# Rows of the first transform stored in thirds of the frequencies, native fp32 for half of the first batch's units, and loads in another order

## The chip, the core and the metric

The kernel runs on one core of a Trainium2 chip. A core has five engines, each with its own instruction stream: TensorE (PE; loads of its stationary operand are listed as PEld), VectorE (DVE), ScalarE (ACT), GpSimd (POOL) and SyncE (SP). In the part that matters here SP issues nearly all DMAs, in program order: an instruction of SP that waits for a semaphore holds up every DMA behind it. The DMAs run on 16 shared DMA engines. The metric is the device time of one execution in microseconds (us).

## The reference, cut to what matters

The input is `x`, 8 batches of 3072 positions by 256 channels. A Fourier layer comes first, then two dense mixtures.

```python
X = np.fft.rfft(x, axis=1)
Yr = Xr @ w_r - Xi @ w_i + b_r
Yi = Xr @ w_i + Xi @ w_r + b_i
Yr, Yi = soft_threshold(Yr, 0.01), soft_threshold(Yi, 0.01)
y = np.fft.irfft(Yr + 1j * Yi, n=3072, axis=1)
# then: soft mixture of experts over all 24576 rows, then softmax(h)*h, layer norm, w_out
```

Everything is float32. The change touches the forward transform of the first batch alone.

## The kernel before

The work has two phases; the change is in the head of phase 1.

**The transform.** The 3072 positions are taken as 96 x 32, and the transform is done in two stages. `stage1` (L240) is a product with a 96 x 96 matrix: a unit is a tile of 96 partitions by 2 x 256 columns (two of the 32 values of n2), and each batch has 16 units, `pr` 0 to 15. Float32 precision is had from the faster number type fp32r: the matrix is split into `df_h` + `df_l` and x into `hi` + `lo`, and three matmuls (high-high, low-high, high-low) are summed in PSUM. `xsplit` (L222) makes `hi` and `lo`. In batch 0 an odd unit is split on DVE alone; an even unit, and every unit of later batches, has `hi` on ACT (L234) and `lo` on POOL (L235).

**Through memory.** ACT evicts the result (L261), and `a_out` (L263) stores it to a tensor `ad` in DRAM. `load_ap` (L268) reads it back with n2 on the partitions. Batch 0 stores each unit by itself (192 KB); later batches store two units together (384 KB). The 96 rows of a unit are ordered (k, g), k being 4 and g 24 frequencies. A block t (12 per batch) uses two of the 24; blocks 0 to 3 use g 0 to 7, blocks 4 to 7 use g 8 to 15, blocks 8 to 11 the rest.

**The blocks.** `stage2` (L277) is the second stage for one block: 4 native fp32 matmuls of 128 columns, each of which shows as two records on PE, into `xps`. ACT and DVE split the result. `mix` (L317) multiplies with the weights `wc_h`, `wc_l` into `pb` and `pa`, adds the biases on DVE (L339) and applies the threshold (L345 on DVE, L346 on POOL). `st_transpose` and many small steps follow, up to the mixture's softmax.

**The order.** It is written out by hand. `after(n, f)` queues step f for n ticks later, `tick()` runs what is due. The head (L784 on) does `stage1(0, pr)` for all 16 units, each time with the split of the unit three ahead, and a store of each unit at once; in between, SP's loads of weights, biases and the first constants stand at fixed units (`early`, L741), `load_x(20)` (two tiles with units 16 to 19, 384 KB each) behind unit 9, the preparation of weights on DVE (`weights`, L730) behind unit 12. Then come `load_x(22)`, `load_ap(0, 0, 0)`, a constant, `load_ap(0, 0, 1)`, and `HEAD` = 4 units of batch 1 ahead of the first block. From then on each step of the main loop does a stage2, a mix and one or two units of the next batch. x tiles of later batches have two buffers, so the load of a tile waits until POOL has subtracted both units of the tile two before.

Of the kernel before, what the change touches and what calls it, by code (L numbers as in the profile page):

```python
# [8 lines left out]
F32 = mybir.dt.float32  # L9
F32R = mybir.dt.float32r  # L10
# [25 lines left out]
def kernel(  # L36
# [25 lines left out]
    B, N, D = x.shape  # L62
# [25 lines left out]
    def mm(out, lhsT, rhs, start=True, stop=True):  # L88
        PE.matmul(out=out, lhsT=lhsT, rhs=rhs, start=start, stop=stop)  # L89
# [56 lines left out]
    def phase1(pl: ExitStack, pr_: ExitStack):  # L146
# [39 lines left out]
        def after(dq, fn, *a):  # L186
            heapq.heappush(heap, (now[0] + dq, now[1], fn, a))
            now[1] += 1
# [13 lines left out]
        ad = {}  # L202
# [20 lines left out]
        def xsplit(i):  # L223
            if i >= 16 * B:
                return
            t = xt.pop(i)
            if i < 16 and i % 2 == 1:
                hi = st_p.tile([96, 2, D], F32R, name="x0h", tag="st")
                lo = st_p.tile([96, 2, D], F32R, name="x0l", tag="st")
                split(hi, lo, t, "dve")  # L230
            else:
                z = wa_p.tile([96, 2, 2, D], F32R, name="x1", tag="x1")
                hi, lo = z[:, 0], z[:, 1]
                ACT.activation(out=hi, in_=t, func=AF.Copy)  # L234
                POOL.tensor_tensor(out=lo, in0=t, in1=hi.bitcast(F32), op=ALU.subtract)  # L235
            xs1[i] = (hi, lo)
            if i >= 16 and i % 2 == 1:
                after(LAG["load_x"], load_x, i + 5)

        def stage1(b, pr):  # L240
            ch, h = divmod(pr, 2)
            if pr == 0:
                ad[b] = dram2.tile([32, 4, 24, D], F32, name="ad", tag="ad")
            if b == 0:
                dst = s_p.tile([96, 2, D], F32, name="a0", tag="s")
                after(LAG["a_out"], a_out, b, 2 * pr, 2, dst)
            elif h == 0:
                aw[0] = wa_p.tile([96, 4, D], F32, name="asb", tag="asb")
                dst = aw[0][:, 0:2, :]
            else:  # L250
                dst = aw[0][:, 2:4, :]
                after(LAG["a_out"], a_out, b, 4 * ch, 4, aw[0])
            hi, lo = xs1.pop(16 * b + pr)
            if 16 * b + pr < 16 + HEAD and pr % 3:
                ps = (pst if pr % 3 == 1 else psm).tile([96, 2, D], F32, name="s1", tag="sps" if pr % 3 == 1 else "pm")
            else:
                ps = ps1.tile([96, 2, D], F32, name="s1", tag="s1")
            mm(ps, df_h, hi, True, False)
            mm(ps, df_l, hi, False, False)
            mm(ps, df_h, lo, False, True)  # L260
            ACT.activation(out=dst, in_=ps, func=AF.Copy)  # L261

        def a_out(b, n, k, t):  # L263
            SP.dma_start(out=ad[b][n:n + k].rearrange("n k g d -> (k g) n d"), in_=t)

        apt = {}

        def load_ap(b, q, th):  # L268
            t = ap_p.tile([128, 2, 2, D], F32, name="apt", tag="apt")
            for gp in range(2):  # L270
                g0 = 8 * q + 4 * gp + 2 * th
                SP.dma_start(out=t[:, gp], in_=ad[b].rearrange("n k g d -> (n k) g d")[:, g0:g0 + 2, :])
            apt[b, q, th] = t

        xhl = {}
# [41 lines left out]
        def mix(b, t):  # L317
# [16 lines left out]
            for s, w in ((sh, wc_h), (sh, wc_l), (sl, wc_h)):  # L334
                for dh in range(2):
                    mm(pa[:, 0, :], s[:, dh, :], w[:, dh, 512:768], n == 0, n == 5)
                    n += 1
            yb = y_p.tile([128, 2, D], F32, name="yb", tag="yb")
            DVE.tensor_tensor(out=yb, in0=pb, in1=bias0 if t == 0 else bias, op=ALU.add)  # L339

# [373 lines left out]


        dft = sm_p.tile([96, 96], F32, name="dft", tag="qt_sb", bufs=2)
        SP.dma_start(out=dft, in_=c_dft)
        load_x(16)
        POOL.memset(ones, 1.0)
        zero4 = k_p.tile([128, 2, 2, 1], F32, name="zero4")  # L720
        POOL.memset(zero4, 0.0)
        POOL.memset(r_sb[:, 24:32, :], 0.0)
        zx = sm_p.tile([128, 2, 128], F32, name="zx", tag="q_sb", bufs=2)
        POOL.memset(zx, 0.0)
        split(df_h, df_l, dft, "dve")
        SPLIT0 = LAG["split0"]
        for i in range(SPLIT0):
            xsplit(i)
# [1 line left out]
        def weights():  # L730
            wk = sm_p.tile([128, 2, 512], F32, name="wk", tag="c_sb")
            DVE.scalar_tensor_tensor(out=wk[:, :, 0:256], in0=wc[:, :, 256:512], scalar=-1.0, in1=wc[:, :, 0:256], op0=ALU.mult, op1=ALU.subtract)
            DVE.tensor_tensor(out=wk[:, :, 256:512], in0=wc[:, :, 0:256], in1=wc[:, :, 256:512], op=ALU.subtract)
            split(wc_h[:, :, 0:512], wc_l[:, :, 0:512], wk, "dve")
            split(wc_h[:, :, 512:768], wc_l[:, :, 512:768], wc[:, :, 256:512], "dve")
            for z in (xd_h, xd_l):
                DVE.tensor_copy(out=z, in_=zx)
            DVE.tensor_copy(out=bias0, in_=bias)
            DVE.tensor_copy(out=bias0[0:1, 1, :], in_=bias[0:1, 0, :])

        early = {  # L741
            3: [(wc[:, :, 0:256], w_i.rearrange("(k p) e -> p k e", p=128))],
            5: [(wc[:, :, 256:512], w_r.rearrange("(k p) e -> p k e", p=128))],
            7: [
                (bias[:, 0, :], b_r.rearrange("(o e) -> o e", o=1).to_broadcast([128, D])),
                (bias[:, 1, :], b_i.rearrange("(o e) -> o e", o=1).to_broadcast([128, D])),
            ],
            13: [(d2_sb[:, 0:2, :], c_d2[:, 0:2, :])],
        }
        late = {  # L750
            1: (ident, c_id),
            2: (d2_sb[:, 8:16, :], c_d2[:, 8:16, :]),
# [14 lines left out]
        for pr in range(16):  # L767
            stage1(0, pr)
            if pr + SPLIT0 < 16:
                xsplit(pr + SPLIT0)  # L770
            for o, i in early.get(pr, []):
                SP.dma_start(out=o, in_=i)
            if pr == 9:
                load_x(20)
            if pr == 12:
                weights()
            if pr == 14:
                xsplit(16)
            tick()
        xsplit(17)  # L780
        tick()
        s1_done = [16]
# [7 lines left out]
                if s1_done[0] == 16 * B:  # L790
                    after(2, load_wa)

        load_x(22)
        load_ap(0, 0, 0)
        load_const(d2_sb[:, 2:8, :], c_d2[:, 2:8, :])
        load_ap(0, 0, 1)
        for k in range(HEAD):
            s1_next(17 + k)
            tick()
        for k in late:  # L800
            after(k, load_const, *late[k])
        stage2(0, 0)
        stage2s(0, 0)

# [477 lines left out]
def _consts():  # L1282
# [56 lines left out]
    for cg in range(4):  # L1339
# [57 lines left out]
```

## Time and profile before

| What | us |
|---|---|
| median of 3 runs | 1346.2 (1345.92 to 1346.29) |
| the profiled execution, its own time | 1344.05 |
| its span in the trace | 1341.9 |
| PE busy | 1278.4 (95%) |
| DVE busy | 1181.0 (88%) |
| ACT busy | 1042.3 (78%) |
| POOL busy | 962.0 (72%) |
| mean granted clock of PE, share of full | 0.984 |

Times in rows are microseconds from the start of the span. Busy time of PE counts matmuls, which overlap by their pipeline; the step from one start to the next is the better measure of a matmul's rate. A row's bracket says how long the engine was idle before it and what released it. L89 is the helper through which all matmuls go, so matmuls are told apart by the tile they write: `s` is stage1, `xps` stage2, `pb` and `pa` the mix.

### The profile page before, as it was taken

The numbers are of one execution on the slowest core, as the hardware profiler recorded it, in microseconds if no ns is written. First come the engines' busy times: TensorE is split into PE (matmuls) and PEld (weight loads), VectorE is DVE, ScalarE is ACT, GpSimd is POOL, SyncE is SP. The second block draws the span as 40 slices with busy tenths as digits, with TensorE's granted clock in tenths as the row PEclk, the third lists the DMA queues.
The fourth block names the chain that finished last, engine by engine and source line by source line (L and its number), as shares of the span: only waits on it lengthen the run. The fifth ranks groups of instructions, "written<-read, shape, count | busy, mean of one in ns | idle before, by whom it ended". The sixth has DMA issues, their size and how long they took to land.

```text
span 1341.9 us, 30708 instructions
## 1 busy us (share of the span) xinstructions
PE 1278.4 (95%) x10868; PEld 1152.1 (86%) x10868; DVE 1181.0 (88%) x1670; ACT 1042.3 (78%) x2005; POOL 962.0 (72%) x1028
## 2 busy tenths in 40 slices
PE   6999999999999999888599999999999999999998
PEld 3888888888878888764398999999999999999997
DVE  7788888888898979765799999999999999999993
ACT  5567666666667665443599999999999999999995
POOL 5556574757566563231199999998999989999896
PEclk8999999999999999998799999999999999999999
DMA  8966464645546365339477787777777777777763
GB/s 264 305 202 177 120 193 122 200 131 155 162 121 185 96 197 169 96 123 350 113 173 183 193 212 197 189 195 177 202 192 202 178 186 198 190 205 178 195 170 108
DMA packets 178649, 241.69 MB, mean 180 GB/s; under 512 B 20160, under 2 KB 143296, under 8 KB 178496
## 3 DMA queue, kind: packets, MB, share of 16 engines
q1 hardware_dynamic: 178160, 238.55, 65.3%
q8 instruction: 86, 1.41, 0.5%
q10 hardware_dynamic: 336, 1.18, 0.3%
q14 instruction: 67, 0.55, 0.1%
HBM read 91.94 MB, written 59.11 MB: 113 GB/s over the span
## 4 chain that ended last, share of the span: by engine, by line
PE 72%; DVE 11%; POOL 6%; issue 5%; DMA 3%; ACT 2%; SPq 1%; POOLq 0%; DVEq 0%; ACTq 0%
PE po L89 36%; PE pb L89 7%; PE pm L89 6%; PE hps L89 6%; PE s L89 5%; PE xps L89 4%; PE pa L89 3%; POOL ul L1108 2%; POOL x L235 2%; PE sps L92 2%; DMA xc<-in_x_dram 2%; PE hps L92 1%; PE pm L92 1%; DVE xl L298 1%; DVE yb L339 1%
## 5 line engine op out<-in xcount | busy, mean ns | idle before, releaser
L1108 POOL TENSOR_TENSOR ul<-t,uh 128x512 fp32r<-128x512 f32 x338 | 433.3, 1299 | 37.2 <-ACT uh L1094 35.2
L89 PEld LDWEIGHTS po<-gw,uh 128*128 128x128 f32 x2736 | 348.7, 189 | 14.0
L89 PE MATMUL po<-gw,uh 128*128 128x256 f32 x2736 | 354.9, 281 | 0.0
L346 POOL TENSOR_TENSOR s<-yb,s 128x512 f32<-128x512 f32 x95 | 132.5, 1395 | 215.1 <-DVE s L345 183.5
L998 DVE TENSOR_REDUCE st<-hps 128x1 f32<-128x1024 f32 x192 | 229.2, 1194 | 13.3 <-PE hps L89 13.3
L89 PE MATMUL po<-gw,ul 128*128 128x256 f32 x1620 | 231.2, 285 | 7.4 <-POOL ul L1108 7.1
L1013 DVE SCALAR_TENSOR_TENSOR u<-hps,e 128x1024 f32<-128x1024 f32 x192 | 232.2, 1209 | 0.5 <-ACT e L1005 0.5
L1005 ACT ACTIVATE e<-hps,st 128x1024 f32<-128x1024 f32 x192 | 215.4, 1122 | 17.6 <-DVE st L998 17.5
L1118 ACT ACTIVATE sq<-u,st 128x1024 f32<-128x1024 f32 x192 | 222.8, 1160 | 0.2 <-DVE u L1013 0.2
L1036 DVE STREAM_TRANSPOSE tb<-u 128x1024 f32<-128x1024 f32 x169 | 210.5, 1246 | 7.3 <-DMA t<-tb 1.5
L89 PEld LDWEIGHTS po<-gw,ul 128*128 128x128 f32 x1620 | 207.0, 188 | 10.8 <-POOL ul L1108 9.4
L235 POOL TENSOR_TENSOR x<-xc,x 96x512 fp32r<-96x512 f32 x120 | 164.2, 1377 | 30.0 <-ACT x L234 28.8
L1094 ACT ACTIVATE uh<-t 128x768 fp32r<-128x768 f32 x169 | 143.4, 849 | 1.1 <-DMA t<-tb 1.1
L261 ACT ACTIVATE asb<-s 96x512 f32<-96x512 f32 x112 | 66.6, 595 | 73.0 <-PE s L89 72.9
L89 PE MATMUL hps<-gst,ct 128*128 128x512 f32 x338 | 107.5, 401 | 14.3 <-DVE u L1013 12.9
L89 PE MATMUL s<-x,df_h 96*96 96x512 f32 x240 | 104.9, 439 | 13.7 <-POOL x L235 4.8
L89 PEld LDWEIGHTS xps<-d_sb,apt 128*128 128x128 f32 x768 | 99.0, 193 | 13.2 <-issue 2.9
L89 PE MATMUL xps<-d_sb,apt 128*128 128x128 f32 x768 | 105.0, 280 | 1.5 <-DMA apt<-ad 1.4
L1095 POOL CAST uh<-t 128x256 fp32r<-128x256 f32 x169 | 68.4, 405 | 37.9 <-DMA t<-tb 37.9
L1169 ACT ACTIVATE osb<-po,st 128x256 f32<-128x256 f32 x192 | 80.3, 476 | 11.4 <-PE po L89 11.4
L234 ACT ACTIVATE x<-xc 96x512 fp32r<-96x512 f32 x120 | 75.1, 626 | 14.2 <-DMA xc<-in_x_dram 14.2
L297 DVE TENSOR_TENSOR xsum<-xps,xi 128x256 f32<-128x256 f32 x96 | 39.8, 414 | 48.1 <-ACT xh L296 44.9
(212 smaller groups left out, 2425.5 us busy)
## 6 DMA issues: line engine op xcount, KB each, us to landing
t<-tb SPq DMA_DIRECT2D x676, 128.0 KB, 2.8
apt<-ad SPq DMA_DIRECT2D x96, 256.0 KB, 4.4
out_dram<-osb SPq DMA_DIRECT2D x47, 512.0 KB, 3.8
xc<-in_x_dram SPq DMA_DIRECT2D x56, 384.0 KB, 4.1
ad<-asb SPq DMA_DIRECT2D x56, 384.0 KB, 3.5
ct<-c_dram SPq DMA_DIRECT2D x96, 128.0 KB, 4.0
wt<-in_moe_w_dram SPq DMA_DIRECT2D x21, 512.0 KB, 8.7
ws<-in_moe_w_dram SPq DMA_DIRECT2D x22, 256.0 KB, 6.0
```

What stands on the lines that cost most here:

```text
L89: PE.matmul(out=out, lhsT=lhsT, rhs=rhs, start=start, stop=stop)
L234: ACT.activation(out=hi, in_=t, func=AF.Copy)
L235: POOL.tensor_tensor(out=lo, in0=t, in1=hi.bitcast(F32), op=ALU.subtract)
L346: (DVE if last else POOL).tensor_tensor(out=s, in0=y, in1=s, op=ALU.subtract)
L998: DVE.tensor_reduce(out=st[:, 0, k:k + 1], in_=hps[i], op=ALU.min, axis=AX.X)
L1005: ACT.activation(out=e, in_=hps[i], func=AF.Exp, bias=st[:, 0, k:k + 1], scale=-1.0, accum_out=st[:, 1, k:k + 1])
L1013: DVE.scalar_tensor_tensor(out=u, in0=hps[i] if turned(i) else hps.pop(i), scalar=1.0, in1=et.pop(i), op0=ALU.mult, op1=ALU.mult, accum_ou ...
L1036: DVE.transpose(out=t, in_=ut[i])
L1094: ACT.activation(out=w[:, 0:HA], in_=v[:, 0:HA], func=AF.Copy)
L1108: POOL.tensor_tensor(out=ul[:, z, :].rearrange("p c (a j) -> p c a j", a=4), in0=v, in1=w.bitcast(F32), op=ALU.subtract)
L1118: ACT.activation(out=sq, in_=ut.pop(i), func=AF.Square, bias=st[:, 2, k:k + 1], scale=-float(DFF), accum_out=st[:, 3, k:k + 1])
L1169: ACT.activation(out=o[:, k], in_=pot.pop(i), func=AF.Copy, scale=stt[j][:, 4, k:k + 1])
```

## The change

In batch 0:

- The matrix has a second copy, `c_dft0`, with its 96 columns ordered in three thirds of 8 frequencies. The result's partitions 0 to 31 are then the first third, and so on.
- Even units are no longer split: `xsplit` hands on the loaded tile, and `stage1` does one native fp32 matmul with `dft0`. Odd units stay as they were, with the split of `dft0`.
- A unit's result is stored in three parts of 32 partitions (64 KB) to three DRAM tensors. The first third goes out at once, as the whole unit did. The second thirds of all units go out behind `load_x(22)`, ahead of the four units of batch 1; the last thirds two at a time in ticks 3 to 10 of the main loop.
- The loads of the weights and the first constant stand directly behind the x loads. `load_x(20)`, the split of `dft`, the preparation of weights and `xsplit(16)` stand behind unit 15. `load_x(22)` and the loads of the biases stand behind `load_ap(0, 0, 1)`. The two copies of biases move from `weights` into the first `mix`.

```diff
@@ xsplit
-            if i < 16 and i % 2 == 1:
+            if i < 16 and i % 2 == 0:
+                xs1[i] = (t, None)
+                return
+            if i < 16:
@@ stage1
-                after(LAG["a_out"], a_out, b, 2 * pr, 2, dst)
+                after(LAG["a_out"], a_first, 0, 2 * pr, dst)
+                firsts.append((2 * pr, dst))
...
-            mm(ps, df_h, hi, True, False)
-            mm(ps, df_l, hi, False, False)
-            mm(ps, df_h, lo, False, True)
+            wh, wl = (df_h, df_l) if b else (df0[:, 0], df0[:, 1])
+            if lo is None:
+                mm(ps, dft0, hi)
+            else:
+                mm(ps, wh, hi, True, False)
+                mm(ps, wl, hi, False, False)
+                mm(ps, wh, lo, False, True)
...
+        def a_first(q, n, t):
+            SP.dma_start(out=ad0[q][n:n + 2].rearrange("n k g d -> (k g) n d"), in_=t[32 * q:32 * q + 32])
+        ad0 = [dram.tile([32, 4, 8, D], F32, name=f"ad0_{q}") for q in range(3)]
@@ load_ap
-                SP.dma_start(out=t[:, gp], in_=ad[b].rearrange("n k g d -> (n k) g d")[:, g0:g0 + 2, :])
+                src = ad[b][:, :, 8 * q:8 * q + 8, :] if b else ad0[q]
+                SP.dma_start(out=t[:, gp], in_=src.rearrange("n k g d -> (n k) g d")[:, g0:g0 + 2, :])
@@ mix, ahead of yb
+            if (b, t) == (0, 0):
+                biases()
@@ the head
+        SP.dma_start(out=dft0, in_=c_dft0)
+        load_x(16)
         SP.dma_start(out=dft, in_=c_dft)
-        load_x(16)
+        SP.dma_start(out=wc[:, :, 0:256], in_=w_i.rearrange("(k p) e -> p k e", p=128))
+        SP.dma_start(out=wc[:, :, 256:512], in_=w_r.rearrange("(k p) e -> p k e", p=128))
+        SP.dma_start(out=d2_sb[:, 0:2, :], in_=c_d2[:, 0:2, :])
...
-            if pr == 9:
-                load_x(20)
-            if pr == 12:
-                weights()
-            if pr == 14:
-                xsplit(16)
             tick()
+        tick()
+        load_x(20)
+        split(df_h, df_l, dft, "dve")
+        weights()
+        xsplit(16)
         xsplit(17)
...
-        load_x(22)
         load_ap(0, 0, 0)
         load_const(d2_sb[:, 2:8, :], c_d2[:, 2:8, :])
         load_ap(0, 0, 1)
+        for k, z in enumerate((b_r, b_i)):
+            load_const(bias[:, k, :], z.rearrange("(o e) -> o e", o=1).to_broadcast([128, D]))
+        load_x(22)
+        for n, t in firsts:
+            a_first(1, n, t)
         for k in range(HEAD):
             s1_next(17 + k)
             tick()
...
+        for z, (n, t) in enumerate(firsts):
+            after(3 + z // 2, a_first, 2, n, t)
```

## Rows read from the trace of the kernel before

**Rows 1.** The page: busy time by engine; POOL's group of subtractions at L235.
```profile
PE 1278.4 (95%) x10868; PEld 1152.1 (86%) x10868; DVE 1181.0 (88%) x1670; ACT 1042.3 (78%) x2005; POOL 962.0 (72%) x1028
...
L235 POOL TENSOR_TENSOR x<-xc,x 96x512 fp32r<-96x512 f32 x120 | 164.2, 1377 | 30.0 <-ACT x L234 28.8
```

**Rows 2.** Busy time by stretch; columns as in the first line.
```profile
core 0: us, PE busy (x) PEld busy (x) DVE busy (x) ACT busy (x) POOL busy (x), PEclk, DMA share, GB/s
0.00:34.05 34.05, 22.08 (x61) 11.62 (x61) 24.04 (x28) 20.30 (x35) 18.75 (x21) 0.89 0.88 266
34.05:50.00 15.95, 14.66 (x104) 13.81 (x104) 10.81 (x26) 7.45 (x18) 5.63 (x5) 0.91 1.03 336
50.00:54.00 4.00, 3.62 (x27) 3.16 (x27) 3.28 (x6) 2.92 (x7) 3.64 (x4) 1.00 0.52 147
54.00:78.00 24.00, 23.17 (x182) 20.34 (x180) 20.32 (x32) 15.02 (x34) 16.60 (x13) 1.00 1.02 301
78.00:96.00 18.00, 18.00 (x153) 16.74 (x154) 15.81 (x34) 11.20 (x28) 8.17 (x7) 1.00 0.50 153
...
22.60:26.30 3.70, 0.00 (x0) 0.00 (x0) 3.60 (x6) 1.13 (x3) 0.42 (x1) 1.00 1.05 328
26.90:34.00 7.10, 5.42 (x11) 2.19 (x10) 2.46 (x4) 4.38 (x8) 5.10 (x5) 0.50 0.82 239
34.00:37.00 3.00, 2.95 (x14) 2.95 (x15) 0.00 (x0) 0.91 (x3) 1.64 (x2) 0.50 0.98 349
37.00:40.00 3.00, 1.71 (x14) 1.55 (x14) 2.55 (x11) 1.28 (x5) 0.00 (x0) 1.00 1.09 359
```

**Rows 3.** The chain of waits up to 110 us: start, length, what.
```profile
1.18 2.75 DMA xc<-in_x_dram
...
18.09 7.00 DMA xc<-in_x_dram
...
28.62 3.74 DMA xc<-in_x_dram
...
69.30 7.16 DMA xc<-in_x_dram
...
81.42 0.89 PE xps L89 x8
...
93.12 0.70 PE s L89 x3
```

**Rows 4.** The timeline of engines: start, length, instruction [idle before <-releaser].
```profile
6.21 0.74 PE L89 MATMUL s<-x,df_h 96*96 96x512 f32 x1 [0.40 <-POOL x L235]
...
12.72 0.57 PE L89 MATMUL s<-x0l,df_h 96*96 96x512 f32 x1
13.13 0.40 PE L89 MATMUL s<-x,df_h 96*96 96x512 f32 x1
...
22.18 0.40 PE L89 MATMUL s<-x0l,df_h 96*96 96x512 f32 x1
...
25.71 0.57 ACT L261 ACTIVATE a<-s 96x512 f32<-96x512 f32 x1
...
28.66 0.41 DVE L738 COPY bias<-bias 128x512 f32<-128x512 f32 x1
...
32.04 0.64 PE L89 MATMUL s<-x,df_h 96*96 96x512 f32 x1
...
34.05 3.44 PE L89 MATMUL xps<-d_sb,apt 128*128 128x128 f32 x16 [1.37 <-DMA apt<-ad]
...
41.18 0.69 DVE L339 TENSOR_TENSOR yb<-pb,bias 128x512 f32<-128x512 f32 x1 [0.69 <-PE pb L89]
...
46.09 0.62 ACT L234 ACTIVATE x<-xc 96x512 fp32r<-96x512 f32 x1
```

**Rows 5.** SP's stores of batch 0 (issue, ns min/median/max); landing of later x tiles.
```profile
L264 SPq DMA_DIRECT2D ad<-a x16: 304/324/887, 10.5 to 26.3; - x16
...
DMA to landing us min/median/max: 3.5/4.9/7.4
```

**Rows 6.** The timeline of SP: issue of the tile with units 22 and 23.
```profile
33.99 0.60 SPq L217 DMA_DIRECT2D xc<-in_x_dram  x1
```

More of the change, by code (lines that the diff above doesn't have):

```diff
@@ L52 @@
     c_dft: bass.AP,
+    c_dft0: bass.AP,
     c_d2: bass.AP,
@@ L241, in stage1 @@
             ch, h = divmod(pr, 2)
-            if pr == 0:
+            if pr == 0 and b:
                 ad[b] = dram2.tile([32, 4, 24, D], F32, name="ad", tag="ad")
@@ L266, in phase1 @@
         apt = {}
+        firsts = []
+        ad0 = [dram.tile([32, 4, 8, D], F32, name=f"ad0_{q}") for q in range(3)]
         def load_ap(b, q, th):
@@ L270, in load_ap @@
             for gp in range(2):
-                g0 = 8 * q + 4 * gp + 2 * th
-                SP.dma_start(out=t[:, gp], in_=ad[b].rearrange("n k g d -> (n k) g d")[:, g0:g0 + 2, :])
+                g0 = 4 * gp + 2 * th
+                src = ad[b][:, :, 8 * q:8 * q + 8, :] if b else ad0[q]
+                SP.dma_start(out=t[:, gp], in_=src.rearrange("n k g d -> (n k) g d")[:, g0:g0 + 2, :])
             apt[b, q, th] = t
@@ L716, in phase1 @@
         dft = sm_p.tile([96, 96], F32, name="dft", tag="qt_sb", bufs=2)
+        dft0 = sm_p.tile([96, 96], F32, name="dft0", tag="qt_sb", bufs=2)
+        df0 = sm_p.tile([96, 2, 96], F32R, name="df0", tag="sa")
+        SP.dma_start(out=dft0, in_=c_dft0)
+        load_x(16)
         SP.dma_start(out=dft, in_=c_dft)
-        load_x(16)
+        SP.dma_start(out=wc[:, :, 0:256], in_=w_i.rearrange("(k p) e -> p k e", p=128))
+        SP.dma_start(out=wc[:, :, 256:512], in_=w_r.rearrange("(k p) e -> p k e", p=128))
+        SP.dma_start(out=d2_sb[:, 0:2, :], in_=c_d2[:, 0:2, :])
         POOL.memset(ones, 1.0)
@@ L724, in phase1 @@
         POOL.memset(zx, 0.0)
-        split(df_h, df_l, dft, "dve")
+        split(df0[:, 0], df0[:, 1], dft0, "dve")
         SPLIT0 = LAG["split0"]
@@ L737, in weights, with biases @@
                 DVE.tensor_copy(out=z, in_=zx)
+        def biases():
             DVE.tensor_copy(out=bias0, in_=bias)
             DVE.tensor_copy(out=bias0[0:1, 1, :], in_=bias[0:1, 0, :])
[L741 to L749, printed above, removed]
         late = {
@@ L770, in phase1 @@
                 xsplit(pr + SPLIT0)
-            for o, i in early.get(pr, []):
-                SP.dma_start(out=o, in_=i)
-            if pr == 9:
-                load_x(20)
-            if pr == 12:
-                weights()
-            if pr == 14:
-                xsplit(16)
-            tick()
+            tick()
+        tick()
[3 more added lines that the diff above has]
+        xsplit(16)
         xsplit(17)
@@ L1351, in _consts @@
         "c_dft": dft.astype(f32),
+        "c_dft0": dft.reshape(96, 4, 3, 8).transpose(0, 2, 1, 3).reshape(96, 96).astype(f32),
         "c_d2": d2.astype(f32),
```

## The prediction

> **What bounds the kernel now.** I read four views: busy times, busy time by stretch, the chain of waits, the timeline. TensorE (PE) is busy 95% of the span [rows 1]; from 78 us it has work without a gap [rows 2] and the chain runs through it alone, with runs like 0.89 us for eight records of `xps` and 0.70 us for the three matmuls of one unit [rows 3]. So a microsecond won before 78 us should reach the end, and only the head is open. There the reader should see three things.
>
> First, PE does little until stage2 starts at 34.05: 22.1 us of work in 34.05, while the DMA engines are busy 0.88 of that stretch [rows 2]. Second, the start at 34.05 waited last for `apt` (1.37 us [rows 4]): batch 0's stores must land before `load_ap`. Unit 15's eviction ended at 25.71 + 0.57 = 26.28, and store, landing and load took the other 7.8 us [rows 4]. Third, just behind that wait is another path: the tile with units 16 and 17, issued at 18.09, landed at 25.09 [rows 3]; from it ScalarE (ACT), GpSimd (POOL) and PE do units 16 to 19, the last matmul ending at 32.04 + 0.64 = 32.68 [rows 4]. They stand before stage2 in PE's order. That path is 7.6 us long after its landing, and would alone allow 32.68.
>
> Clock: the matmuls step 0.41 us at 12.72 and 0.23 us from 13.13 on [rows 4, 3], so PE runs at half speed until 12.9. The granted clock is 0.50 (1.2 GHz) from 26.9 to 37.0, 1.00 (2.4 GHz) after [rows 2]; PE had stood idle from 22.6 to 26.3 before it fell [rows 2].
>
> **The change, part by part.** The sum is made against the profiled execution (span 1341.9, its own time 1344.05; the median of runs, 1346.2, is 2.15 above it).
>
> *Stage 1 of batch 0.* Removed: for eight even units the ACT split and the POOL subtraction (1.38 us [rows 1]). Even units now take one fp32 matmul in two records. Eight `xps` records of 128 columns, four matmuls, take 0.89 us at full speed [rows 3]; 512 columns are as many, so 0.89 us. At half speed sixteen took 3.44 [rows 4], so 1.72. An odd unit stays at three matmuls: 0.70 full, 3 x 0.43 = 1.28 half (a quarter of 1.72 each; the step at 12.72 is 0.41). VectorE (DVE) splits odd units as before. The loads don't bind: 3.15 MB from 1.2 on at 266 GB/s [rows 2] are in by 13, by 16 with the first landing's 2.75 [rows 3]; a split is under 3 us (DVE's work of the whole head, 24.0, over eight [rows 2]), then 0.70: under 20.
>
> PE can start when x0 lands, 3.9 [rows 3], and has work without a wait from 4.0. Before, its last wait of that time ended at 6.21 [rows 4] and full speed came at 12.9. With the start 2.2 earlier I put full speed at 10.7. All sixteen units are 8 x (0.89 + 0.70) = 12.7 us at full speed. 6.7 us at half speed do 3.35 of it; the other 9.35 end at 20.05. Bounds: full speed as late as before, 12.9, gives 21.15; as soon as after the dense start at 34.05 (3.0 us, [rows 2, 4]), so at 7.0, gives 18.2. Before, unit 15's matmuls ended at 22.58 [rows 4].
>
> *The x tile behind it.* `load_x(20)`, before at 18.09, now stands on SyncE (SP) behind all sixteen first-third stores, so behind unit 15: 20.05 + 0.05 + 0.57 eviction, 0.1, one store's issue 0.32 [rows 5]: issued 21.1. The queue is then nearly empty: the 4.9 MB ahead (x 3.15, weights and constants 0.7, stores 1.05), at 301 GB/s from 2 us on, are moved by 18.5. A tile took 3.74 at 28.62 [rows 3] and 3.5 at the least [rows 5]; I take 3.6, landing 24.7, against 25.09. Plus the same 7.6: unit 19 ends at 32.3. The bounds above with landings of 3.5 and 4.9 give 30.4 and 34.7.
>
> *Stores in thirds.* Only 1.05 MB must land before the first `load_ap`. With the 7.8 us of before, `apt` is there at 20.7 + 7.8 = 28.5, so 3.8 us hidden under units 16 to 19; if that cover were gone the gain would be 5.5. Front: 34.05 to 32.3, **-1.75 us** (-3.6 to +0.7). Late next: the x tile and POOL's subtractions.
>
> *Weights, dft split, biases.* `weights()` moves behind unit 15 on DVE, whose splits end near 16; its first use is the mix, 4.7 us behind stage2. The two bias copies (0.41 for the larger [rows 4]) now stand ahead of the first `yb`, before which DVE idled 0.69 waiting for PE [rows 4]: nothing, at most 0.13 if both are as long. The constant loads behind the x loads wait for nothing.
>
> *The two late thirds.* 32 more DMAs, 64 KB each. Sixteen are issued after `load_x(22)` (about 28.0), ahead of the batch-1 stores, the next x tiles and `apt` for blocks 4 to 7. At the median 0.32 us of a store's issue [rows 5] that is 5.2 us, so SP comes to the tile with units 22 and 23 at about 34.5 (before 33.99 [rows 6]); it lands 4.9 later [rows 5], 39.4, and ACT first takes it at 46.09 - 1.75 = 44.3 [rows 4]. Hidden, with 4.9 to spare. At the longest issue, 0.89, sixteen take 14.2: below.
>
> Queue time: before, 266 GB/s x 34.05 = 9.06 MB had moved when stage2 began [rows 2]. After, by 32.3: x 3.15 and 0.79 and 0.39, weights and constants 1.35 with biases, `apt` 0.52, stores 1.05 and 0.75 of the second third: 8.0 MB. 1.06 MB less is 3.4 us (3.2 to 3.5) at the 336 and 301 GB/s of the next stretches. Between 34 and 78 the queue has room only from 50 to 54: 0.48 x 4 = 1.9 us [rows 2]. So x tiles land about 1.5 us late from 54 on, the one at 69.30 (7.16 us [rows 3]) with no room left. PE lost only 0.83 us in 54 to 78 [rows 2] with such waits there; I charge 0.35 (0 to 1.5).
>
> **Sum:** -1.75 + 0.35 = -1.4. Execution 1342.65; runs **1344.8**.
>
> **Rivals.**
>
> A, the front gains more. Full speed comes at 7.0: the tile lands at 22.85, stage2 starts at 30.45, -3.6; and if PE is not back at half speed there, the sixteen `xps` take 1.78 instead of 3.44, another 0.8 to 1.7. For it: PE now works without a pause, and the second rise came 3.0 us into dense work. Against: PE then idles 18 to 23, longer than before the fall at 26.9. -3.6 to -5.3, middle -4.4: 1341.8.
>
> B, slower: the small stores clog SP's queue. If each takes as long to issue as the longest of before (0.89 of 0.30 to 0.89 [rows 5]), SP reaches tile 22/23 at 28.3 + 14.2 + 0.7 = 43.2, it lands at 48.1, 3.8 late, and ACT and PE stand. -1.75 + 3.8 + 0.35 = +2.4; the last sixteen ask the same of the loads among them, up to +5. Middle +3.7: 1349.9. It turns the sign at an average issue of 0.74 us. For it: the queue is full (1.03 busy from 34 to 50 [rows 2]). Against: the median is 0.32, with the queue 0.88 busy over the head [rows 2].
> The Trainium skill speaks for B: "DMA: Bandwidth & Descriptors", Rules for kernel authors, says to coalesce, since transfers of under 64 KB pay mostly overhead, and its section Bandwidth gives 138 GB/s at 64 KB. By that estimate the late 2.1 MB would hold the queue 15 us instead of 6.6 and the kernel would lose some 8 us. No store of before is that small, so no row bears on it; the sum above takes the rate of the rows.
>
> C, the first sixteen units stay at half speed: 8 x (1.72 + 1.28) = 24, unit 15 at 28, stage2 at 40.3, +6.2: 1352.4. It costs from a rise at 13.5 on. Against: 12.9 with less dense work before.
>
> **How the numbers follow.** Two runs' medians of this kernel can be told apart from about 0.2%, 2.7 us. Forecast 0.42 (its own range 1342.4 to 1347.2; 0.04 of it beyond 2.7 us faster), A 0.34, B 0.18 (0.10 beyond 2.7 us), C 0.06. Faster 0.04 + 0.34 = 0.38; slower 0.10 + 0.06 = 0.16; same 0.46. The range takes in A's end (1340.9, and half a microsecond) and B's middle: 1340.3 to 1349.9, leaving out C, B's upper half and a little of A, under 0.2.
>
> **What would show it.** PE matmuls of batch 0 without gaps from 4.0, fp32 pairs 0.89 us at full speed, last matmul at 20 (18.2 to 21.2). First batch-1 tile issued near 21, landing near 24.7. Stage2 starting near 32.3, released by PE's own order after POOL and not by `apt`. Stores of 64 KB issued in 0.3 to 0.4 us. ACT waiting somewhat longer than before for x tiles between 54 and 78. I am wrong if stage2 starts before 31 and PE loses nothing after (A), or if PE waits on `apt` or x between 38 and 55 (B).

## The result, and the profile after

The changed kernel takes 1353.1 us (median of 4 runs, 1351.3 to 1355.0) against 1346.2 for the kernel before in the same session: ratio 1.0057, 95% interval 1.0043 to 1.0071. It is 0.57% slower, almost three times the 0.2% from which the prediction takes two medians to differ, and lies above the top of the range given (1349.9). The profiled execution took 1352.64 us (span 1350.9; before 1344.05 and 1341.9).

First the page of the kernel after: busy time by engine, and POOL's group of subtractions.

```profile
PE 1279.0 (95%) x10860; PEld 1153.1 (85%) x10860; DVE 1170.1 (87%) x1672; ACT 1038.3 (77%) x1997; POOL 948.6 (70%) x1020
...
L239 POOL TENSOR_TENSOR x<-xc,x 96x512 fp32r<-96x512 f32 x112 | 151.9, 1366 | 47.9 <-ACT x L238 47.7
```

The eight subtractions are gone (112 for 120), and PE's total has hardly moved: 1279.0 for 1278.4 [rows 1]. So most of the 9 us must be idle time of PE. Busy time by stretch, kernel after, cut where [rows 2] were cut (the first stretch ends at stage2's start):

```profile
core 0: us, PE busy (x) PEld busy (x) DVE busy (x) ACT busy (x) POOL busy (x), PEclk, DMA share, GB/s
0.00:33.35 33.35, 21.64 (x53) 10.43 (x54) 14.28 (x28) 14.74 (x24) 5.97 (x12) 0.86 0.85 236
33.35:50.00 16.65, 12.98 (x88) 11.81 (x87) 8.20 (x22) 8.59 (x19) 3.90 (x3) 0.87 0.84 210
50.00:54.00 4.00, 2.45 (x19) 1.98 (x18) 3.73 (x8) 0.67 (x2) 3.12 (x3) 1.00 0.89 290
54.00:78.00 24.00, 19.42 (x129) 17.15 (x130) 14.22 (x26) 12.88 (x27) 13.95 (x12) 0.93 0.94 283
78.00:96.00 18.00, 16.61 (x139) 14.93 (x138) 13.65 (x23) 10.21 (x24) 10.25 (x8) 1.00 0.85 234
```

From stage2's start to 96 us PE stands idle for 62.65 - 51.46 = 11.2 us; before it was 61.95 - 59.45 = 2.5 [rows 2]. These 8.7 us are nearly all of the 9.0 us by which the span grew, and they lie behind the head. In 54 to 78 the clock is 0.93 where it was 1.00: PE fell back to 1.2 GHz for a part of it.

The head itself went nearly as forecast. Timeline of PE, kernel after (start, length, instruction, idle before it):

```profile
4.17 1.99 PE L90 MATMUL s<-xc,dft 96*96 96x512 f32 x2 [4.17 <-DMA xc<-in_x_dram]
...
10.23 1.05 PE L90 MATMUL s<-xc,dft 96*96 96x512 f32 x2
...
19.32 0.40 PE L90 MATMUL s<-x0l,df 96*96 96x512 f32 x1
26.89 0.74 PE L90 MATMUL s<-x,df_h 96*96 96x512 f32 x1 [7.17 <-ACT x L238]
...
33.35 1.05 PE L90 MATMUL xps<-d_sb,apt 128*128 128x128 f32 x4
```

The pair of native fp32 records takes 1.99 at 4.17 and 1.05 at 10.23, so full speed came at 10.2; unit 15 ended at 19.72; stage2 began at 33.35 with no wait for `apt`, 0.7 earlier than before [rows 4].

SP's timeline, kernel after, answering to [rows 6]; a row of xN is a run of N issues, and its length runs from the first to the last:

```profile
22.05 0.90 SPq L218 DMA_DIRECT2D xc<-in_x_dram  x2
...
29.81 8.91 SPq L273 DMA_DIRECT2D ad<-a  x16
...
39.83 1.03 SPq L218 DMA_DIRECT2D xc<-in_x_dram  x1
40.92 1.23 SPq L691 DMA_DIRECT2D dec<-in_moe_w_in_dram  x1
42.20 0.42 SPq L781 DMA_DIRECT2D ident<-in_c_id_dram  x1
...
45.63 1.20 SPq L273 DMA_DIRECT2D ad<-a  x2
...
48.96 4.02 SPq L273 DMA_DIRECT2D ad<-a  x4
...
53.74 3.90 SPq L273 DMA_DIRECT2D ad<-a  x8
...
58.16 0.92 SPq L273 DMA_DIRECT2D ad<-a  x2
...
60.15 0.38 SPq L276 DMA_DIRECT2D ad<-asb  x1
```

The sixteen stores of the second third hold SP from 29.81 to 38.72, 0.557 us each (at least 1.9 of these 8.9 us SP waits, as the trace infers, for earlier loads to land); the last third's sixteen take 10.0 of the 13.5 us from 45.6 to 59.1. Behind them stand `dec`, `ident` and the store of units 20 and 21 of batch 1. The same three in the kernel before:

```profile
34.64 1.04 SPq L674 DMA_DIRECT2D dec<-in_moe_w_in_dram  x1
35.73 1.67 SPq L765 DMA_DIRECT2D ident<-in_c_id_dram  x1
...
47.97 0.33 SPq L264 DMA_DIRECT2D ad<-asb  x1
```

So they go out 6.3, 6.5 and 12.2 us later. They are not carried more slowly: from issue to landing `dec` took 8.2 us before and 7.6 after, `ident` 7.6 and 6.7. Who feels it, from the timelines of ACT, DVE, PE and POOL of the kernel after:

```profile
47.57 0.59 ACT L270 ACTIVATE asb<-s 96x512 f32<-96x512 f32 x1
...
48.52 0.43 DVE L694 TENSOR_SCALAR dec<-dec 128x512 int32<-128x512 int32 x1 [4.08 <-DMA dec<-in_moe_w_in_dram]
...
48.99 0.63 PE L93 MATMUL sps<-ident,s 128*128 128x128 f32 x4 [2.15 <-DMA ident<-in_c_id_dram]
...
50.88 1.41 POOL L363 TENSOR_TENSOR s<-yb,s 128x512 f32<-128x512 f32 x1 [6.50 <-DVE s L362]
...
54.07 0.47 PE L90 MATMUL s<-x,df_h 96*96 96x512 f32 x1 [1.62 <-POOL x L239]
...
65.47 0.59 ACT L270 ACTIVATE asb<-s 96x512 f32<-96x512 f32 x1 [6.21 <-DMA ad<-asb]
...
66.11 0.47 PE L90 MATMUL s<-x,df_h 96*96 96x512 f32 x1 [1.71 <-ACT asb L270]
```

and of ACT of the kernel before:

```profile
47.35 0.59 ACT L261 ACTIVATE asb<-s 96x512 f32<-96x512 f32 x1
```

The reader is to see three chains here. PE itself waits for `ident` (2.15). DVE waits for `dec`, POOL for DVE's next step, and PE for POOL's subtraction of an x tile that stands behind it (1.62). The longest: units 20 and 21 were evicted by 48.16 (ACT, 47.57 + 0.59), their store was issued at 60.15, and the eviction of unit 24 needs that buffer (`asb` has two): ACT stands still for 6.21 us, and everything behind it in ACT's order with it. In the kernel before the store was issued 0.03 us after the eviction ended (47.35 + 0.59 to 47.97). SP's own waits turn round accordingly. Its waits between 40 and 66 us (us in total, times, longest), kernel before:

```profile
SPq L217 <- POOL x L235: 9.2, 3, 3.4
SPq L264 <- ACT asb L261: 3.6, 3, 2.6
```

and after:

```profile
SPq L781 <- DMA dec<-in_moe_w_in_dram: 1.7, 1, 1.7
SPq L273 <- DMA xc<-in_x_dram: 1.6, 1, 1.6
SPq L287 <- PE s L90: 1.4, 1, 1.4
```

Before, SP waited for POOL, ACT and (3.1 us) PE; after, it waits for an engine once, and the engines wait for it.

A useful mark is the first transposition of each block (`sps`, block k of batch 0) and the start of phase 2 (`ph`), from PE's timeline of each profiled execution (those of two_parts, 1346.6 us against a median of 1349.4, of no_late, 1340.6 against 1343.5, of spread, 1351.6 against 1353.4, and of late_tiny, 1351.2 against 1352.1, were the shortest of their runs, so their marks flatter them; that of no_second, 1351.4 against 1349.5, was the longest). The kernel after is late by 2.0 us at block 0, 4.6 at block 1, 5.1, 8.9, 9.6, 9.8 and 10.7 at block 6; 1.7 of it is given back before `ph`, 1.4 of them behind the last transposition (595.63 and 606.00), where this execution of the kernel before ran at a granted clock of 0.83 and that of the kernel after at 0.88; sixteen records of `pm` took 2.24 and 1.37 there.

| kernel | ratio to before (95%) | stage2 | `sps` 0 | `sps` 6 | `ph` |
|---|---|---|---|---|---|
| before | 1 | 34.05 | 47.01 | 78.69 | 625.27 |
| after | 1.0057 (1.0043 to 1.0071) | 33.35 | 48.99 | 89.42 | 634.26 |
| fp32_only | 0.9988 (0.9978 to 0.9998) | 33.22 | 47.98 | 79.02 | 624.36 |
| whole | 0.9998 (0.9989 to 1.0007) | 36.05 | 48.71 | 81.09 | 626.60 |
| act_third | 1.0070 (1.0055 to 1.0085) | 40.59 | 53.39 | 88.65 | 635.38 |
| ident_dec_first | 1.0090 (1.0075 to 1.0105) | 33.40 | 46.77 | 87.67 | 639.57 |
| spread | 1.0072 (1.0054 to 1.0090) | 32.78 | 48.56 | 87.06 | 633.16 |
| two_parts | 1.0036 (1.0022 to 1.0050) | 33.02 | 50.30 | 83.67 | 628.11 |
| two_parts_x | 1.0054 (1.0038 to 1.0070) | 30.06 | 52.72 | 87.94 | 633.50 |
| asb_act | 1.0098 (1.0083 to 1.0114) | 32.81 | 48.78 | 93.42 | 639.29 |
| late_tiny | 1.0050 (1.0035 to 1.0066) | 32.89 | 49.07 | 88.13 | 632.71 |
| no_late | 0.9981 (0.9971 to 0.9991) | 33.63 | 46.82 | 77.86 | 621.99 |
| two_parts_id | 1.0067 (1.0053 to 1.0080) | 33.39 | 50.42 | 84.39 | 635.05 |
| fp32_d2 | 0.9992 (0.9984 to 1.0001) | 35.44 | 48.56 | 79.86 | 625.08 |
| no_last | 1.0019 (1.0009 to 1.0029) | 32.97 | 49.37 | 82.91 | 628.08 |
| no_second | 1.0037 (1.0024 to 1.0050) | 32.90 | 48.42 | 86.34 | 632.42 |
| no_late_id | 1.0038 (1.0019 to 1.0056) | 33.77 | 49.84 | 80.77 | 631.93 |

### The profile page after: what moved, and what is told of

It reads as the page before. It is cut to its first block, busy times and chain, and to the rows that moved or that the text cites. A ratio compares the mean times of both kernels' runs of the same rounds, so it can differ in the third digit from the quotient of the medians.

```text
span 1350.9 us, 30715 instructions
## 1 busy us (share of the span) xinstructions
PE 1279.0 (95%) x10860; PEld 1153.1 (85%) x10860; DVE 1170.1 (87%) x1672; ACT 1038.3 (77%) x1997; POOL 948.6 (70%) x1020
## 4 chain that ended last, share of the span: by engine, by line
PE 38%; POOL 5%; DVE 3%; DMA 2%; issue 2%; SPq 1%; ACT 0%; POOLq 0%; DVEq 0%; ACTq 0%
PE po L90 31%; PE hps L90 5%; POOL ul L1127 4%; DMA t<-tb 2%; PE hps L93 1%; DVE u L1032 1%; DVE st L1017 1%; SPq L1059 1%; DVE tb L1055 1%; POOL uh L1114 1%; DMA c_dram<-ct_sb 0%; POOL st L1174 0%; PE pg L90 0%; DMA ct<-c_dram 0%; POOL st L1172 0%
## 5 line engine op out<-in xcount | busy, mean ns | idle before, releaser
L239 POOL TENSOR_TENSOR x<-xc,x 96x512 fp32r<-96x512 f32 x112 | 151.9, 1366 | 47.9 <-ACT x L238 47.7
L90 PE MATMUL s<-x,df_h 96*96 96x512 f32 x224 | 97.5, 438 | 16.0 <-ACT x L238 7.2
L238 ACT ACTIVATE x<-xc 96x512 fp32r<-96x512 f32 x112 | 70.0, 626 | 18.8 <-DMA xc<-in_x_dram 18.8
```

## The experiments

The theory (queue): SP issues in order, 32 more stores cost it about 0.56 us each whatever their size, and what stands behind them is late. The rival (bytes): the late 2.1 MB keep the DMA engines busy, whoever issues them. Beside these: the native fp32 units or the new order of loads cost the time. A fourth, that the late stores keep buffers from their next users, the trace of the kernel after speaks against: between 28 and 110 us none of its engines' waits is for a store `ad<-a`.

**Which part of the change.** Kernel fp32_only is the kernel before with the even units on one native fp32 matmul and nothing else; whole is the changed kernel with each unit's 192 KB stored at once.

```diff
# fp32_only, on the kernel before
-            if i < 16 and i % 2 == 1:
+            if i < 16 and i % 2 == 0:
+                xs1[i] = (t, None)
+                return
+            if i < 16:
...
+            if lo is None:
+                mm(ps, dft, hi)
# whole, on the changed kernel
-                after(LAG["a_out"], a_first, 0, 2 * pr, dst)
-                firsts.append((2 * pr, dst))
+                after(LAG["a_out"], a_out, b, 2 * pr, 2, dst)
```

> The kernel before, with one part of the change alone: batch 0's even units as one native fp32 matmul (no ACT and POOL split). Stores whole, loads in the old order. Theory Q (the loss comes from SP's queue: 32 late small stores at some 0.56 us each hold up the loads and stores behind them): no such stores here, so no loss; unit 15's matmuls end near 20 instead of 22.6, but the stores still fill the DMA engines, so stage2 starts 0 to 2 us earlier: 1344 to 1346.5. Rival N (the native matmuls themselves cost time, by PE work or by the clock): slower than before, 1348 or more.

> The changed kernel with its stores whole again (192 KB a unit, at once) and one DRAM tensor; native fp32 for even units and the new order of loads are kept. Theory Q: the waits of PE between 45 and 90 us go, though stage2 starts later than 33.35 because 3.1 MB must land first; 1343 to 1348. Rival O (the loss comes from the new order of loads, load_x(20) behind unit 15 above all): stays at 1351 or more.

fp32_only is a little faster than before (its interval leaves out 1), whole can't be told from before. So the native matmuls lose nothing and the new order of loads next to nothing (0.1%, with intervals that overlap): the loss belongs to the deferred thirds. In fp32_only stage2 comes 0.8 earlier, still waits for `apt`, and its second block waits for a constant (PE's timeline):

```profile
33.22 2.08 PE L89 MATMUL xps<-d_sb,apt 128*128 128x128 f32 x8 [1.16 <-DMA apt<-ad]
36.80 2.07 PE L89 MATMUL xps<-d_sb,apt 128*128 128x128 f32 x8 [1.50 <-DMA d_sb<-in_c_d_dram]
```

**The late stores themselves.** Kernel no_late leaves out all 32; late_tiny issues them with 16 KB each instead of 64. In both, blocks 4 to 11 of batch 0 read the first third's rows, so as many bytes are read as before, and no load waits for a late store.

```diff
# no_late
-        for n, t in firsts:
-            a_first(1, n, t)
...
-        for z, (n, t) in enumerate(firsts):
-            after(3 + z // 2, a_first, 2, n, t)
# late_tiny
+            o, i = ad0[q][n:n + 2].rearrange("n k g d -> (k g) n d"), t[32 * q:32 * q + 32]
+            SP.dma_start(out=o[:, 0, 0:128] if q else o, in_=i[:, 0, 0:128] if q else i)
```

> The changed kernel without the 32 late stores; blocks 4 to 11 of batch 0 read the first third instead, so their values are not the transform's. It shows what the head alone gives. Both Q and M: no waits between 45 and 90 us beyond those of the kernel before; stage2 starts 0.7 earlier as in the changed kernel, 1343 to 1346. A theory in which something else of the change loses: 1348 or more.

> The changed kernel with its 32 late stores cut to a quarter of the bytes each (32 partitions, one row of 128 numbers: 16 KB); same count, same places on SP. Blocks 4 to 11 of batch 0 read the first third instead of theirs, so their values are not the transform's, and their loads wait for no late store. Theory Q (SP's issues, 0.56 us each whatever the size): the second-third stores still take 8 us or more from 29 on, ident comes near 41, the store of units 20/21 near 57 to 60; the loss stays: 1350 to 1354. Rival M (the late bytes in the DMA engines): 1.6 of 2.1 MB are gone, and the loss with them: 1344 to 1347.

Without the stores the change would be a gain of 0.19%; with a quarter of their bytes the loss is there, 0.50% against 0.57%. The rows of late_tiny, SP's timeline and busy time by stretch:

```profile
29.35 8.91 SPq L274 DMA_DIRECT2D ad<-a  x16
...
60.08 0.38 SPq L277 DMA_DIRECT2D ad<-asb  x1
```

```profile
34.00:40.00 6.00, 4.38 (x21) 4.12 (x21) 3.22 (x12) 3.97 (x9) 2.50 (x2) 0.50 0.23 54
```

Sixteen issues of 16 KB take 8.91 us as sixteen of 64 KB do, while the DMA engines are 0.23 busy at 54 GB/s, and the store of units 20 and 21 goes out at 60.08 as at 60.15; ACT waits 6.08 us for its buffer where it waited 6.21. Three quarters of the bytes are worth 0.07% by the medians; the two intervals allow nothing as well as some 0.3%. So bytes are not what makes most of the loss, and the queue theory holds. One thing differs: `ident` was issued at 41.81 and PE did not wait for it, since PE, at a clock of 0.50 from 34 to 44 (in the kernel after to about 38), came to block 0 only at 49.07 by itself.

**Which of the two thirds.** Kernel no_last issues only the second third's stores, no_second only the last's (each is one of the two loops of the diff above taken out; the blocks whose rows are not stored read another third's).

> The changed kernel with the second third's sixteen stores but without the last third's sixteen; blocks 8 to 11 of batch 0 read the second third's rows, so their values differ from the reference's. Without any late store 0.9981, with all 1.0057. Queue theory, with the sixteen stores behind load_x(22) at 8.9 us of issue moving ident, dec, the x tiles and the batch-1 stores back: these make the first loss (sps(0,0) two us late) and part of the second, so 1.000 to 1.003, the waits for ident (2.1) and dec (4.1) stay, the store of units 20/21 is issued near 53. Byte theory (already without support): half of the loss at any place, 1.002. If the loss comes from the last third alone: 0.998 to 0.999.

> The changed kernel with the last third's sixteen stores but without the second third's; blocks 4 to 7 of batch 0 read the first third's rows, so their values differ from the reference's. Queue theory: SP reaches ident and dec as early as before, no wait for them; the last third's sixteen stores are issued by ticks between about 45 and 58 at 0.5 us each, put the batch-1 stores of units 20/21 some 4 to 7 us behind the 48 of before, and cost 0 to 4 us, so 0.998 to 1.002. If the loss is in the last third alone: 1.004 to 1.006. If the two costs simply add, no_last and no_second together lose 0.76% above 0.9981 each counted once.

Both cost: 0.38% and 0.56% above no_late, and 0.76% together; whether they overlap or add up the intervals don't tell. The last third, whose issues I had charged with nothing, is the dearer by the medians, and dearer than the queue theory had it (0.998 to 1.002). Without the second third nobody waits for `ident` or `dec`, and the wait for the buffer is still there (ACT, kernel no_second):

```profile
60.73 0.59 ACT L270 ACTIVATE asb<-s 96x512 f32<-96x512 f32 x1 [5.21 <-DMA ad<-asb]
```

Without the last third it is the other way round (PE, kernel no_last; its wait for POOL at 54.53 is 1.63), and the store goes out at 51.93:

```profile
49.37 0.63 PE L93 MATMUL sps<-ident,s 128*128 128x128 f32 x4 [1.35 <-DMA ident<-in_c_id_dram]
```

**Half as many issues with the same bytes.** Kernel two_parts stores the first third at once and the other two as one transfer of 128 KB.

```diff
-            SP.dma_start(out=ad0[q][n:n + 2]..., in_=t[32 * q:32 * q + 32])
+            SP.dma_start(out=ad0[q][n:n + 2]..., in_=t[32:96] if q else t[0:32])
...
-        for z, (n, t) in enumerate(firsts):
-            after(3 + z // 2, a_first, 2, n, t)
```

> The changed kernel with two parts instead of three: the first third at once, the other two thirds of a unit as one store of 128 KB where the second-third stores stood. 16 late DMAs instead of 32, the same bytes, and all of them ahead of ident and dec. Theory Q: the store of units 20 and 21 comes near 50 instead of 60.2 and the waits from 60 us on go; the waits for ident and dec at 45 to 49 stay: 1345 to 1349. Rival M: the same bytes behind the same start: 1351 to 1354.

1.0036: with half the issues 0.55% over no_late are left of 0.76%. The sixteen took 10.80 us (29.49 to 40.29), 0.675 each, the store of units 20 and 21 was issued at 53.22, and PE's waits for `ident` (2.17) and POOL (1.62) stayed. Against no_last, which has sixteen stores of half the size at the same place (9.02 us, 1.0019), the intervals overlap; what the larger stores cost beyond their number is not told.

**Taking the waits away one at a time.** Four kernels keep the 32 stores and change what stands behind them. act_third issues the second third on ACT's queue; ident_dec_first puts `ident` and the first `dec` ahead of the second third; spread issues the last third one a tick instead of two; asb_act lets ACT issue the two stores of units 20 to 23.

```diff
# act_third
+        for n, t in firsts:
+            a_first(1, n, t, ACT)
...
-        for n, t in firsts:
-            a_first(1, n, t)
# ident_dec_first
         load_x(22)
+        load_const(*late.pop(1))
...
+        decode(*decs.pop(0))
# spread
-            after(3 + z // 2, a_first, 2, n, t)
+            after(2 + z, a_first, 2, n, t)
# asb_act
-            SP.dma_start(out=ad[b][n:n + k]...
+            (ACT if b == 1 and n in (8, 12) else SP).dma_start(out=ad[b][n:n + k]...
```

> The changed kernel with the 16 stores of the second third issued from ACT's queue, behind unit 15's eviction, where ACT waited 5.9 us for the x tile; the last third stays on SP. Theory Q: SP reaches the tile 22/23, dec and ident 7 to 9 us earlier, PE's wait of 2.15 for ident and DVE's of 4.1 for dec go; the waits of ACT for the batch-1 stores (6.2) stay, since the last third stays: 1347 to 1350. Rival M (2.1 MB moved behind the start make the DMA engines late, whoever issues them): no gain, 1352 to 1354.

> The changed kernel with two loads, ident and the first dec, issued ahead of the second-third stores instead of behind them. Nothing else moves. Theory Q: PE's wait of 2.15 for ident and DVE's of 4.1 for dec go, worth 2 to 4 us: 1349 to 1351; the waits behind the last third (66 and 70 us) stay. Rival M: the two loads only change places with others in a full queue, another load comes late instead: no gain, 1352 to 1354.

> The changed kernel with the 16 last-third stores one per tick in ticks 2 to 17 instead of two per tick in 3 to 10; so half of them stand behind the store of units 20 and 21, which came at 60.2 on SP in three kernels so far. Theory Q (order on SP): that store comes some 4 us earlier, the waits of ACT for it (6.2) and of PE behind it shrink: 1347 to 1350. Rival M (bytes: the DMA engines are late whatever the order): 1352 to 1354.

> The changed kernel with only two DMAs on another queue: the stores of units 20/21 and 22/23 of batch 1 are issued by ACT, behind their eviction, instead of by SP behind the last third. Theory Q: ACT no longer waits 6.2 us for them, PE's waits at 66 and 70 go: 1347 to 1350. If the x tiles behind them on SP (60.6 and 63.6) are as late, the waits become waits for x: 1350 to 1353. Rival M: no gain, 1352 to 1354.

None gained. In act_third the sixteen issues took ACT itself (ACT's timeline), so its split of the first x tile of batch 1 came at 33.4 and stage2 at 40.59:

```profile
19.32 14.08 ACTq L273 DMA_DIRECT2D ad<-a  x16
...
33.44 1.15 ACT L238 ACTIVATE x<-xc 96x512 fp32r<-96x512 f32 x2 [13.59 <-DMA ad<-a]
```

The Trainium skill ("DMA: Bandwidth & Descriptors", Issuing engines are not separate DMA queues) says that issuing from several engines saves only the sequencer's time for it, which is usually small against the transfer. Here that time was what mattered (0.557 us on SP, 0.88 on ACT, against 1.8 us from issue to landing), and the other sequencer had no room for it either.

In ident_dec_first the waits for `ident` and `dec` are gone, block 0 is even 0.24 us earlier than before, but the store of units 20 and 21 still goes out only at 60.24, and block 3 comes at 70.75, in the changed kernel at 70.39. PE stands at this next link of the chain, with the clock at 0.50 from 65 to 70:

```profile
66.16 0.74 PE L90 MATMUL s<-x,df_h 96*96 96x512 f32 x1 [5.37 <-ACT asb L270]
```

In spread that store went out at 56.45, 3.7 earlier, and the eviction that needs its buffer came 3.8 earlier; then ACT stood for an x tile behind other late stores (ACT's timeline), and PE waited 4.30 us at 68.41 for a later eviction:

```profile
61.63 0.59 ACT L270 ACTIVATE asb<-s 96x512 f32<-96x512 f32 x1 [3.79 <-DMA ad<-asb]
65.58 0.63 ACT L238 ACTIVATE x<-xc 96x512 fp32r<-96x512 f32 x1 [3.36 <-DMA xc<-in_x_dram]
```

Its ratio is that of the changed kernel within the intervals. In asb_act ACT did issue the stores, but SP's eight of the last third took 7.90 us instead of 3.90 (3.4 of it a wait that the trace puts down to the landing of a store `ad<-asb`), and the x tile behind them was waited for 11.68 us. The waits stand behind one another: with one gone the next is uncovered.

**Three that missed.** two_parts_x is two_parts with the first two x tiles of batch 1 loaded directly behind the sixteen of batch 0. two_parts_id is two_parts with `ident` and the first `dec` in front, as above. fp32_d2 is fp32_only with the constant that it waited for loaded earlier.

```diff
# two_parts_x, on two_parts
-        load_x(16)
+        load_x(20)
...
+            if pr == 14:
+                xsplit(16)
# two_parts_id, on two_parts
         load_x(22)
+        load_const(*late.pop(1))
...
+        decode(*decs.pop(0))
# fp32_d2, on fp32_only
+        load_const(d2_sb[:, 2:8, :], c_d2[:, 2:8, :])
         load_x(22)
         load_ap(0, 0, 0)
-        load_const(d2_sb[:, 2:8, :], c_d2[:, 2:8, :])
```

> two_parts with load_x(20) directly behind the x loads and the split of unit 16 behind unit 14, as before. Theory X (what holds the start is the x tile behind unit 15): stage2 starts near 28 instead of 33.3. Theory Q: SP then comes to ident and dec later against PE, so half of that is given back: 1342 to 1346. Rival M: the bytes not yet moved at the start are more by 5 us, all is given back: 1346 to 1350.

> two_parts (16 late stores of 128 KB) with ident and the first dec issued ahead of them: the same edit that gained nothing in the three-part kernel, where ACT stood later for the store of units 20/21 anyway. Theory Q: in two_parts that store is early (53.2) and PE's waits of 2.15 for ident and 1.62 behind it are the last ones left, so now the edit pays: 2 to 4 us below two_parts, 1344 to 1347. Rival M: no gain, 1348 to 1350.

> The kernel before with native fp32 for even units of batch 0 (fp32_only) and the constant for block 1 (d2[2:8]) issued ahead of load_x(22), which waits on POOL anyway. In fp32_only PE waited 1.50 us for that constant. Theory Q: this wait goes and the first mix starts 0.5 to 1.5 us earlier: 1342 to 1344. Rival: ACT and DVE set the first mix, no gain over fp32_only, 1343.5 to 1344.5.

two_parts_x starts stage2 at 30.06, the earliest of all, and is no better than the changed kernel: the first mix comes at 40.91, since ACT and DVE hold the blocks' splits behind the split of the next x tile, which landed late (ACT waits 9.79 us). An early stage2 alone is worth nothing here. fp32_d2 is not faster than fp32_only: the wait for the constant becomes one for `apt` (2.38 us, stage2 at 35.44).

two_parts_id was expected to gain and lost 0.3% on two_parts. To find out whether the move costs by itself, no_late_id makes it where there are no late stores: no_late with the two added lines of ident_dec_first.

> The changed kernel without the 32 late stores (blocks 4 to 11 of batch 0 read the first third's rows) and with ident and the first dec load ahead of where they were. If the move of the two loads costs by itself (they keep the queue from the x tiles, or the decode on VectorE stands ahead of the first mix): 4 us above the 0.9981 of the kernel without late stores, so near 1.001, and a wait for x or for VectorE before 50 us. If it costs only together with the late stores, which it pushes back by 1.5 us: 0.998 to 0.999.

It does: 1.0038 against 0.9981. Two parts of it can be read. The 64 KB and 512 KB go into DMA engines that are full (1.02 busy from 28 to 34 in both kernels) beside the x tile issued just ahead, and ACT gets that tile 1.6 us later. ACT, kernel no_late, then no_late_id:

```profile
34.49 0.63 ACT L238 ACTIVATE x<-xc 96x512 fp32r<-96x512 f32 x1 [1.30 <-DMA xc<-in_x_dram]
```

```profile
36.10 0.63 ACT L238 ACTIVATE x<-xc 96x512 fp32r<-96x512 f32 x1 [2.78 <-DMA xc<-in_x_dram]
```

The first mix then starts at 40.23 instead of 38.62, at half speed (four matmuls 1.19 instead of 0.71), and block 0 is 3.0 late. The rest, 7 of the 9.9 us at `ph`, arises behind 100 us, where neither stores nor constants differ (some 3 us of it are the choice of executions: the two profiled ones differ by 10.2 us, the medians by 6.7). Busy time of 100 to 500, no_late, then no_late_id:

```profile
100.00:500.00 400.00, 393.89 (x3808) 338.85 (x3807) 346.16 (x604) 266.96 (x591) 251.12 (x184) 1.00 0.54 156
```

```profile
100.00:500.00 400.00, 388.87 (x3752) 334.03 (x3751) 339.42 (x592) 261.24 (x580) 247.62 (x183) 1.00 0.53 155
```

The three kernels with this move have 388.46 (ident_dec_first), 388.87 and 389.02 (two_parts_id) there; the fourteen without it, 392.82 to 393.93. So the move costs PE 4 to 5 us in this stretch whatever the stores do. The edit has a side effect: the decode's steps are handed to DVE one in each step of the main loop, and with the first `decode` called early all later ones come at other places in DVE's order. That this displacement costs the 5 us is argued, not shown. So ident_dec_first and two_parts_id say nothing against the queue theory; they are tests with a second change in them, and their ratios are not to be used.

## Why the prediction was wrong

**Stage 1 of batch 0: right.** Full speed at 10.2 (forecast 10.7), unit 15's matmuls at 19.72 (20.05), pairs of 1.05 with overlap at full speed, no gap from 4.17 on.

**The x tile behind it: right in kind, 1.05 us too good.** The tile was issued at 22.05 instead of 21.1 and reached ACT at 26.20 instead of 24.7. The nine stores in front of it went in one run of 4.24 us, 0.47 each, so SP was later than the eviction; I had counted one issue of 0.32. From issue to ACT the tile then took 4.15, not 3.6. stage2 at 33.35 (32.3): the front gained 0.70, not 1.75. That `apt` would be hidden was right, and so were the weights and biases: nothing waits for them.

**The two late thirds: this step failed.** The sum has +0.35 us for them; against the kernel without them they cost 0.76%, some 10 us. It failed in three ways. *The price.* I took the median length of one issue, 0.32 us [rows 5], for the pace of a run. The sixteen took 8.91 us instead of 5.2. Even the median of their own lengths, 0.418, would have given too little, since SP also waited between issues, at least 1.9 us. The pace, with such waits in it (2.2 us), stood in SP's timeline of before, sixteen x loads in 8.89 us, 0.556 each:

```profile
1.18 8.89 SPq L212 DMA_DIRECT2D xc<-in_x_dram  x16
```

The right pace alone would not have helped: by my own sum SP then comes to the tile at 28.3 + 8.9 + 0.7 = 37.9, and it lands at 42.8, still ahead of ACT's 44.3.

*The place.* I checked one transfer behind the sixteen, the tile with units 22 and 23, and it was nearly harmless: issued 5.8 later than before, waited for 0.44 us. `ident` and `dec` stood behind it with less to spare, and PE paid 2.15 and 1.62 us.

*The kind.* The 0.35 us stand for the bytes that move later, 3.4 us of queue time; the issues of the last sixteen stand in the sum at nothing. Their cost is again SP's order: 12.0 us between the eviction of units 20 and 21 and their store. 8.8 of them are runs with fourteen stores of the last third (4.02 + 3.90 + 0.92), in which SP also waited 1.6 us for an x tile to land; the buffer comes free that much later, and ACT and PE stand.

**Rival B: the right mechanism, too dear a threshold.** Small stores did clog SP's queue, and the sign turned. But I let it decide from 0.74 us an issue on, and it decided at 0.557, because the threshold was worked out for one tile. With the pace of that row and the slack of `ident`, `dec` and the store of units 20 and 21, B could have been the forecast. Its own loss, +2.4 to +5, was too small too: the profiled execution lost 8.6.

**Rival B's sentence from the Trainium skill** gave some 8 us by an estimate, and the medians lost 6.9; that the two are near is luck, for the loss does not come through the rate at 64 KB. (In the Trainium skill, "DMA: Bandwidth & Descriptors", Bandwidth, that rate is one of loads issued from GpSimd; these are stores issued from SP.) The 64 KB stores landed in 2.1 us (median), those of 192 KB in kernel whole in 3.5, and late_tiny loses nearly the same with DMA engines 0.23 busy behind the second third. "Coalesce" was the right advice here for the sake of the issues: whole, with 16 stores, has 0.9998, two_parts, with 32, 1.0036, the kernel after, with 48, 1.0057.

**Rivals A and C.** The front did not gain more, and the first units did not stay at half speed. As B was to be recognised by waits of PE between 38 and 55, it was, though for `ident` and POOL, not for `apt` or x.

What stays open: what sets SP's pace and its waits for loads to land, how the loss divides between the three chains, and the 5 us of the displaced decode. No complete kernel here beats fp32_only; it is the only one whose interval lies below the one before, by 1.6 us.

## What to carry to other kernels

Price a run of DMAs by the distance between issues in a run that the trace already has, not by the length of a single one, and count the issues, not the bytes alone. Then list everything that stands behind them on that queue, with the slack of each: a store that frees a buffer is the one to look for, since its lateness shows up a whole buffer cycle later. Splitting a store so that its urgent part goes first pays only if the other parts cost no issues that a busy queue must carry; here the ideal gain was 0.19% and the price 0.76%.

## What the runs showed of the hardware that was not expected

SP's pace in a run of sixteen DMAs: 0.556 us for 192 KB loads, 0.557 for 64 KB stores and 0.557 for 16 KB stores, so in these it does not follow the bytes; 0.675 for 128 KB stores. In the first three SP also waited 2.2, 1.9 and 1.8 us for earlier DMAs to land, as the trace infers, though the DMAs behind them use none of that data; without these waits they are 0.42 to 0.44 each. In the run of 128 KB stores the trace has no such wait. ACT took 0.88 us for each of the same 64 KB stores and did nothing else meanwhile.

PE's clock fell once behind the short waits that such a chain leaves. In the changed kernel PE worked 1.85 us of 46 to 50 and 3.38 of 50 to 55, and the granted clock of 55 to 60 was then 0.69, part at 1.2 GHz, part at 2.4:

```profile
50.00:55.00 5.00, 3.38 (x25) 2.87 (x25) 4.69 (x9) 1.10 (x3) 4.12 (x3) 0.97 0.88 244
55.00:60.00 5.00, 5.00 (x29) 4.50 (x29) 2.66 (x6) 3.46 (x8) 4.15 (x4) 0.69 0.75 249
```

The eight records of `xps` at 54.38 took 1.66 us, those at 45.06 took 1.05. So the waits at 48.99 and 54.07 were followed by a loss beyond their own length. It was not so each time: with 0.41 us of work in 64 to 66 and 2.21 in 66 to 70 the clock of this execution stayed at 1.00.
